# Block means of v moved by products with a shifted identity, and v's rows on other partitions

## The chip, the core and the metric

The kernel runs on one core of one Trainium2 chip. A core has five engines that run their own instruction streams: TensorE (PE, matrix products; its weight loads are listed as PEld), VectorE (DVE), ScalarE (ACT), GpSimd (POOL) and SyncE (SP), which here only issues DMA transfers. Tiles live in SBUF, which has 128 partitions; products are accumulated in PSUM banks. The metric is device time of one execution in microseconds (us), lower is better.

## The reference, cut to what matters

Three stages follow each other, for batch B = 2 and S = 768 positions.

```
attention, 8 heads of 64:
  k_sum = max of k over blocks of 32 rows      v_sum = mean of v over blocks of 32 rows   (24 blocks)
  local scores: q k^T / 8 where |i - j| < 16, else -1e9
  block scores: q k_sum^T / 8 + log 32
  a = softmax over both together;  attn = a @ [v ; v_sum]
gate:      x = attn, heads side by side (768 x 512)
           gate = sigmoid(causal depthwise convolution of x, 5 taps);  y = (gate * (x @ w_val)) @ w_out
spatial:   h = relu(y @ w_in), split into u and v;  v normalised over its 512 columns
           vs = w_spatial @ v + b;   out = (u * vs) @ w_out2
```

The change concerns `v` and `v_sum` of the attention stage: where their rows lie in SBUF, and how the means come there.

## The kernel before, in words

**Tiles.** All working tiles are "units" of 128 partitions x 1536 floats (6 KB a partition), taken from a set of 32; products use 8 PSUM banks. A pair of heads `n` (eight pairs over both batches) is worked on together, and a pair's queries in two groups of 384, so the attention has 16 steps ("ticks").

**Windows.** Queries come in 12 blocks of 64. For a block, the keys that matter are 96 rows (64 of the block and a halo of 16 at each side), followed by the 24 block means: 120 rows in all. `windows(n)` (L512) builds the k side of this by copies in SBUF, along the free dimension. `load_v(n)` (L528) builds the v side along partitions, by four DMA transfers straight from DRAM: two of 64 rows x 768 floats (192 KB each) to partitions 16 to 79, one of 16 rows x 1472 floats (92 KB) to partitions 0 to 15, and one to partitions 80 to 95. Partitions 96 to 119 take the 24 means of v, repeated for all 12 blocks.

**Means of v.** `reduce_v(m)` (L543) loads 128 blocks of 32 rows (two transfers of 512 KB, the tensor `vn`), adds them up on DVE in six halvings, lets ACT multiply by 1/32, and then moves the 128 rows of means by small DMA transfers from SBUF to SBUF (24 rows x 64 floats, fewer at a border) into a staging tile on partitions 96 to 119. It runs three times, with 18 such transfers. `put_vsum(n)` (L564) lets POOL copy a pair's means from the staging tile to its v tile, repeated for the 12 blocks (24 x 1536).

**Attention step.** `scores(t)` (L573): 24 instructions of 64x120 on PE, masking and row maximum on DVE, exponential on ACT, normalisation on POOL. `a_T(t)`: six transposes on PE, a copy on ACT. `pv(t)` (L619): 24 instructions of 120x64 on PE against the v tile; then ACT and DVE split the result into two float32r parts and run the convolution.

**The rest.** All dense products run in float32r as three products of high and low parts (`mm3`, `product`). The weights arrive as doubles in 512 KB pieces and are turned into two parts by ACT, DVE and POOL (`load64`, `split64`). `w_product` multiplies `w_out` by `w_in` ahead of use: two sets (second half of `w_in` first) of 48 products of 128x512 each ("wp"). The gate's products (`val`, 128x384) start when the first ticks of a group are done; then follow `u`, `v`, the spatial product (`s`) and the output (`r`).

**What sets the order.** The functions don't issue instructions; they record them. `ORDER` is a table of steps that sets their priority, and a planner (`plan`, L215) lays all recorded instructions out, engine by engine, by its table of costs, the sharing of units and banks, and the priority. Each engine then runs its list strictly in order, SP's DMA issues included; an instruction whose inputs are not there holds all that stand behind it on its engine. Because a helper issues every instruction, all of them carry one line number in the profile (L213); they are told apart by tile name and shape.

## Time and profile before

| | |
|---|---|
| median of 3 runs | 276.63 us (276.42 to 277.43) |
| profiled execution | 274.73 us |
| its span, from first to last instruction | 273.0 us |
| busy: PE / PEld | 250.0 us (92%) / 224.9 us (82%) |
| busy: DVE / ACT / POOL | 187.8 / 162.4 / 173.8 us |
| moved by DMA | 33.30 MB |

The profiled execution is 1.9 us under the median of the runs. In the profile, idle time of an engine counts only where the end depends on it; the chain of waits, followed back from the last instruction, says where that is. The columns of a stretch are busy time by engine, then the granted clock of TensorE as a share of its full 2.4 GHz, the mean busy share of the 16 DMA engines and the rate that they moved. A matmul's mean duration is longer than what it adds to the busy time, since matmuls overlap in the pipeline; busy time divided by the count is what one costs.

### The profile page before, as it was taken

How to read it: one execution, taken by the hardware profiler on the slowest of the kernel's cores; microseconds unless marked ns; L12 is line 12 of the kernel's file. 1: busy time of each engine (PE TensorE's matmuls, PEld its weight loads, DVE VectorE, ACT ScalarE, POOL GpSimd, SP SyncE). 2: the span in 40 equal slices, each digit the busy share in tenths (PEclk: the TensorE clock that was granted, in tenths of full speed). 3: DMA queues.
4: the chain of work that ended last, by engine and by line, in shares of the span. 5: the costliest groups of instructions: out<-in, count | busy, mean ns of one | idle time of the engine just before them, and what ended most of it. 6: DMA issues, size and time to landing. Idle time of an engine off the chain costs nothing.

```text
span 273.0 us, 5484 instructions
## 1 busy us (share of the span) xinstructions
PE 250.0 (92%) x1914; PEld 224.9 (82%) x1914; DVE 187.8 (69%) x533; ACT 162.4 (59%) x442; POOL 173.8 (64%) x202
## 2 busy tenths in 40 slices
PE   0099998797999999999999999999999999999995
PEld 0076686576999899898899999999988989999884
DVE  0797988987999987585998667564085659257200
ACT  3779979868999999977927444213062534313221
POOL 5789865795978699895554897615137595425210
PEclk9999999799999999999999999999999999999999
DMA  6999999279994000303200050000043041201112
GB/s 203 412 406 407 330 237 242 75 206 320 209 297 158 0 0 10 118 0 118 80 1 0 2 192 0 0 4 0 0 156 115 0 170 64 77 0 41 76 65 90
DMA packets 12243, 33.30 MB, mean 122 GB/s; under 512 B 2216, under 2 KB 2488, under 8 KB 12216
## 3 DMA queue, kind: packets, MB, share of 16 engines
q1 hardware_dynamic: 12184, 32.94, 37.1%
q8 instruction: 15, 0.25, 0.4%
q14 instruction: 12, 0.10, 0.1%
q0 software_dynamic: 32, 0.02, 0.1%
HBM read 29.71 MB, written 3.15 MB: 120 GB/s over the span
## 4 chain that ended last, share of the span: by engine, by line
PE 65%; DMA 19%; DVE 8%; ACT 2%; SPq 2%; issue 1%; POOL 1%; POOLq 0%
PE at_ps L213 65%; DVE at_u L213 7%; DMA at_u<-in_v_dram 6%; DMA at_u<-in_moe_w_val_dram 6%; DMA at_u<-in_vn_dram 3%; DMA at_u<-in_moe_w_in_dram 3%; ACT at_u L213 2%; SPq L213 2%; DVE sm L213 1%; POOL at_u L213 1%; DVE km L213 1%; DMA at_u<-at_u 1%; DVE nm L213 0%; ACT xl L213 0%; ACT at_ps L213 0%
## 5 line engine op out<-in xcount | busy, mean ns | idle before, releaser
L213 PE MATMUL at_ps<-at_u,at_u 128*128 128x384 f32 (+4 forms) x1818 | 241.0, 321 | 18.7 <-ACT at_u L213 14.2
L213 PEld LDWEIGHTS at_ps<-at_u,at_u 128*128 128x128 f32 (+2 forms) x1818 | 214.2, 189 | 42.3 <-ACT at_u L213 17.9
L213 POOL TENSOR_TENSOR at_u<-at_u,at_u 128x512 fp32r<-128x512 f32 (+3 forms) x84 | 111.6, 1351 | 67.4 <-ACT at_u L213 60.7
L213 ACT CAST at_u<-at_u 128x512 fp32r<-128x512 f32 (+3 forms) x84 | 51.0, 635 | 53.5 <-DVE at_u L213 48.2
L213 ACT ACTIVATE at_u<-at_u,nm 128x120 f32<-128x120 f32 x96 | 36.7, 396 | 2.0 <-DVE nm L213 2.0
L213 DVE SCALAR_TENSOR_TENSOR at_u<-at_ps,cw,at_u 128x384 f32<-128x384 f32 (+3 forms) x64 | 36.8, 602 | 0.2
L213 ACT ACTIVATE at_u<-at_ps 128x512 f32<-128x512 f32 (+1 forms) x36 | 19.0, 549 | 25.6 <-PE at_ps L213 24.2
L213 POOL TENSOR_TENSOR at_u<-at_u,sm 128x360 f32<-128x360 f32 x32 | 26.2, 842 | 10.2 <-DVE sm L213 6.4
L213 ACT COPY at_u<-at_ps 120x384 f32<-120x384 f32 (+2 forms) x45 | 20.5, 509 | 10.3 <-PE at_ps L213 10.3
L213 DVE TENSOR_TENSOR at_u<-at_u,at_u 128x384 f32<-128x384 f32 (+2 forms) x31 | 24.9, 820 | 2.4 <-DMA at_u<-in_vn_dram 1.8
L213 DVE TENSOR_TENSOR at_u<-at_ps,at_u 128x384 fp32r<-128x384 f32 (+1 forms) x26 | 14.1, 547 | 17.0 <-PE at_ps L213 15.0
L213 DVE CUSTOM_DVE_ANT_0 at_u<-at_ps,mask 128x120 f32<-128x120 f32 x96 | 20.6, 276 | 2.8 <-PE at_ps L213 2.8
L213 POOL COPY at_u<-at_u 128x320 f32<-128x320 f32 (+2 forms) x24 | 18.5, 787 | 2.1 <-DMA at_u<-at_u 1.8
L213 ACT ACTIVATE at_ps<-at_u 128x512 f32<-128x512 f32 x20 | 12.7, 639 | 11.2 <-DMA at_u<-in_moe_w_in_dram 4.4
L213 ACT ACTIVATION_READ_ACCUMULATOR at_u<-at_u,nm 128x1 f32 x96 | 19.3, 201 | 0.0
L213 DVE TENSOR_SCALAR at_u<-at_u 128x512 uint32<-128x512 uint32 (+1 forms) x21 | 13.9, 669 | 5.5 <-DMA at_u<-in_moe_w_in_dram 5.5
L213 DVE TENSOR_TENSOR at_u<-at_ps,bias 128x384 f32<-128x384 f32 x14 | 7.5, 551 | 13.2 <-PE at_ps L213 13.2
L213 DVE BATCH_NORM_STATS2 st<-at_u 128x6 f32<-128x512 f32 x12 | 8.1, 684 | 12.3 <-ACT at_u L213 12.3
L213 DVE TENSOR_TENSOR at_u<-at_u 128x256 f32<-128x256 f32 (+4 forms) x24 | 14.3, 605 | 3.2 <-DMA at_u<-in_moe_w_spatial_dram 3.0
L213 DVE SCALAR_TENSOR_TENSOR at_u<-at_ps,at_u 128x512 uint32<-128x512 uint32 x20 | 13.6, 686 | 1.3 <-ACT at_ps L213 0.3
L213 PE MATMUL at_ps<-ident,at_u 128*120 128x128 f32 x96 | 12.7, 274 | 1.1 <-POOL at_u L213 1.1
L213 PEld LDWEIGHTS at_ps<-ident,at_u 128*120 128x120 f32 x96 | 10.9, 137 | 2.4 <-POOL at_u L213 1.6
(33 smaller groups left out, 112.7 us busy)
## 6 DMA issues: line engine op xcount, KB each, us to landing
at_u<-in_moe_w_spatial_dram SPq DMA_DIRECT2D x12, 384.0 KB
at_u<-in_moe_w_in_dram SPq DMA_DIRECT2D x8, 512.0 KB
at_u<-in_moe_w_out_dram SPq DMA_DIRECT2D x8, 512.0 KB
at_u<-in_k_dram SPq DMA_DIRECT2D x8, 384.0 KB
at_u<-in_q_dram SPq DMA_DIRECT2D x8, 384.0 KB
at_u<-in_vn_dram SPq DMA_DIRECT2D x6, 512.0 KB
at_u<-in_v_dram SPq DMA_DIRECT2D x16, 192.0 KB
out_dram<-at_u SPq DMA_DIRECT2D x11, 256.0 KB
```

What stands on the lines that cost most here:

```text
L213: getattr(real, method)(*[home(x) for x in args], **{k: home(x) for k, x in kw.items()})
```

## The change

**v on other partitions.** The 64 block rows of v go to partitions 32 to 95 instead of 16 to 79. The two halos share partitions 0 to 31, alternating: the 16 rows from the block before on even partitions, the 16 from the block after on odd ones. The k windows and the masks take the same order along their columns.

**Means by products.** The small transfers go. The identity matrix `ident` (128 x 128) becomes `moves` (128 x 264), which holds it in columns 112 to 239; 120 columns of it, taken at an offset, are a shifted identity. `put_vsum` multiplies the sums of 128 blocks by such a piece, which puts the 24 rows of a head on partitions 96 to 119 of a PSUM bank (two products where a head's rows lie in two tiles, 18 in all). ACT multiplies these 24 rows by 1/32 while it copies them to SBUF, and POOL repeats them as before.

**Planner and tiles.** The recorded regions understand a step of two partitions. Three costs in the planner's table are new. There are 33 units instead of 32 (a placeholder that took one is gone). `ORDER` is new as a whole.

```diff
-NU = 32
+NU = 33
@@ ORDER (first of its lines)
-    in0 lk mask in1 lk wout in1 kw mask in0 wp wout*2 lk in1 lq score wp in1 wout wp kw wval lq kw wval in0 lk wp
+    lk wout lk kw lk kw mask wout in1*2 kw wout lk in0 wval lq in1 wout wp lq in1 mask score kw in0 wval score wp lv
...
@@ def cost
+            if rhs.dtype == F32 and outs[0].ap[0][1] > 64:
+                return 4 * cols / 2.4 + 8, None, 0, False
...
-            rate = 130 if run <= 512 else 405 if parts > 96 else 235 if parts > 64 else 215
+            rate = 130 if run <= 512 else 405 if parts > 96 else 235 if parts > 64 else 380 if parts > 16 else 210
...
-    ident = cst([P, P], F32, "ident")
+    moves = cst([P, 264], F32, "moves")
+    ident = moves[:, 112:240]
...
@@ def load_masks
-        pool.memset(ident, 0.0)
-        pool.affine_select(out=ident, in_=ident, pattern=[[-1, P]], compare_op=ALU.not_equal, fill=1.0, base=0, channel_multiplier=1)
+        pool.memset(moves, 0.0)
+        pool.affine_select(out=moves, in_=moves, pattern=[[-1, 264]], compare_op=ALU.not_equal, fill=1.0, base=112, channel_multiplier=1)
@@ def windows
-        copy("kev", kw[:, :, 16:80], kp.rearrange("p (j r) -> p j r", r=QB))
+        copy("kev", kw[:, :, 32:WK], kp.rearrange("p (j r) -> p j r", r=QB))
...
@@ def load_v
-        pool.memset(vw[0:32, :, 0, :], 0.0)
-        pool.memset(vw[64:96, :, NB - 1, :], 0.0)
+        pool.memset(vw[0:32, :, 0 :: NB - 1, :], 0.0)
         src, dst = v[b, p], vw.rearrange("p h j d -> p (h j d)")
         for h in range(2):
-            sp.dma_start(dst[16:80, h * NB * D : (h + 1) * NB * D], src[:, h * NB * D : (h + 1) * NB * D])
-        sp.dma_start(dst[0:16, D:], src[48:64, :-D])
-        sp.dma_start(dst[80:96, :-D], src[0:16, D:])
+            sp.dma_start(dst[32:WK, h * NB * D : (h + 1) * NB * D], src[:, h * NB * D : (h + 1) * NB * D])
+        sp.dma_start(dst[0:32:2, D:], src[48:64, :-D])
+        sp.dma_start(dst[1:32:2, :-D], src[0:16, D:])
@@ def reduce_v
-        mean = t[1][:, :D]
-        act.mul(mean, t[0][:, :D], 1.0 / 32)
-        r = m * P
-        while r < (m + 1) * P:
-            h, n = divmod(r, NS)
-            if h // H not in MS:
-                MS[h // H] = stage.get().rearrange("p (h d) -> p h d", d=D)
-            e = min((m + 1) * P, r - n + NS)
-            sp.dma_start(MS[h // H][WK + n : WK + n + e - r, h % H, :], mean[r - m * P : e - m * P])
-            r = e
+        MS[m] = t[0][:, :D]
@@ def put_vsum
-        need("vsum", ((2 * n + 2) * NS - 1) // P + 1)
-        need("lv", n + 1)
-        pool.tensor_copy(VW[n][WK:KW], MS[b][WK:KW, 2 * p : 2 * p + 2].unsqueeze(2).to_broadcast([NS, 2, NB, D]))
+        last = ((2 * n + 2) * NS - 1) // P
+        need("vsum", last + 1)
+        need("lv", n + 1)
+        need("mask", 2)
+        po = psum()
+        for h in range(2):
+            r = (2 * n + h) * NS
+            tiles = range(r // P, (r + NS - 1) // P + 1)
+            for m in tiles:
+                x = 16 + r - m * P
+                pe.matmul(po[:KW, h * D : (h + 1) * D], moves[:, x : x + KW], MS[m], start=m == tiles[0], stop=m == tiles[-1], skip_group_check=True)
+        st = stage.get()[WK:KW]
+        act.mul(st, po[WK:KW, : 2 * D], 1.0 / 32)
+        pool.tensor_copy(VW[n][WK:KW], st.rearrange("p (h d) -> p h d", d=D).unsqueeze(2).to_broadcast([NS, 2, NB, D]))
```

**The order on SP, at the start.** The first transfers of before (numbers in names are of units and values; `in_moe_w_in` and `in_moe_w_out` are the weights that wp multiplies):

```order
L213 DMA at_u_76_538<-in_moe_w_in_dram 128x1024
L213 DMA at_u_79_540<-in_k_dram 128x768
L213 DMA at_u_80_545<-in_moe_w_in_dram 128x1024
L213 DMA at_u_79_540<-in_k_dram 128x768
L213 DMA at_u_83_551<-in_moe_w_out_dram 128x1024
L213 DMA at_u_86_553<-in_moe_w_in_dram 128x1024
```

And now:

```order
L221 DMA at_u_73_543<-in_k_dram 128x768
L221 DMA at_u_74_545<-in_moe_w_out_dram 128x1024
L221 DMA at_u_73_543<-in_k_dram 128x768
L221 DMA at_u_79_554<-in_k_dram 128x768
L221 DMA at_u_82_559<-in_moe_w_out_dram 128x1024
L221 DMA at_u_85_564<-in_moe_w_in_dram 128x1024
```

The first product of wp needs a piece of the second half of `w_in` (the third transfer before, the sixth now) and the first of `w_out` (the fifth before, the second now).

**The order on SP, between the sums and the loads of v.** Before, the means of the first two sums (units 138 and 149) stand ahead of the fourth load of v (unit 178):

```order
L213 DMA at_u_150_759<-in_v_dram 16x1472 x2
L213 DMA at_u_164_834<-in_v_dram 64x768 x2
L213 DMA at_u_164_834<-in_v_dram 16x1472 x2
L213 DMA at_u_171_952<-in_moe_w_val_dram 128x1024
L213 DMA at_u_176_971<-in_k_dram 128x768
L213 DMA at_u_139_981<-at_u_138_733 24x64 x5
L213 DMA at_u_139_981<-at_u_138_733 8x64
L213 DMA at_u_177_1042<-in_q_dram 128x768
L213 DMA at_u_139_981<-at_u_149_814 16x64
L213 DMA at_u_139_981<-at_u_149_814 24x64 x4
L213 DMA at_u_139_981<-at_u_149_814 16x64
L213 DMA at_u_178_938<-in_v_dram 64x768 x2
```

Now nothing waits for an engine's result there; a first load of v (not shown) stands ahead of the sums' input:

```order
L221 DMA at_u_140_792<-in_vn_dram 128x1024
L221 DMA at_u_141_803<-in_vn_dram 128x1024
L221 DMA at_u_147_808<-in_vn_dram 128x1024
L221 DMA at_u_148_816<-in_vn_dram 128x1024
L221 DMA at_u_173_824<-in_v_dram 64x768 x2
L221 DMA at_u_173_824<-in_v_dram 16x1472 x2
L221 DMA at_u_182_906<-in_moe_w_val_dram 128x1024
L221 DMA at_u_184_924<-in_k_dram 128x768
L221 DMA at_u_185_939<-in_v_dram 64x768 x2
L221 DMA at_u_185_939<-in_v_dram 16x1472 x2
L221 DMA at_u_188_976<-in_v_dram 64x768 x2
L221 DMA at_u_188_976<-in_v_dram 16x1472 x2
```

**The order on PE, around the first step of `pv`** (64x64 against a v tile). Before:

```order
L213 MATMUL at_ps_207_1106<-at_u_78_584,at_u_85_614 128x512
L213 MATMUL at_ps_189_1111<-at_u_174_978,at_u_142_718 64x64 x12
L213 MATMUL at_ps_207_1106<-at_u_78_584,at_u_85_614 128x512 x3
L213 MATMUL at_ps_193_1150<-at_u_174_978,at_u_150_759 64x64 x12
L213 MATMUL at_ps_207_1106<-at_u_93_656,at_u_85_614 128x512
```

Now, with the products with `moves` that wait for the sums in units 140 and 147:

```order
L221 MATMUL at_ps_180_1054<-at_u_139_965,at_u_106_768 128x512 x3
L221 MATMUL at_ps_186_1092<-at_u_140_792,moves 120x64 x2
L221 MATMUL at_ps_191_1096<-at_u_163_995,at_u_133_586 64x64 x12
L221 MATMUL at_ps_200_1116<-at_u_97_697,at_u_76_608 128x512 x3
L221 MATMUL at_ps_186_1092<-at_u_147_808,moves 120x64
L221 MATMUL at_ps_190_1130<-at_u_147_808,moves 120x64 x2
L221 MATMUL at_ps_200_1116<-at_u_97_697,at_u_76_608 128x512
```

Nine of the 18 products with `moves` stand up to here, two more some 80 rows of the list later, and seven after the last scores.

## Rows read from the trace of the kernel before

**Rows 1.** Stretches: length, busy us (instructions) by engine, clock, DMA share, GB/s:

```profile
0.00:13.20 13.20, 0.00 (x0) 0.00 (x0) 5.68 (x9) 7.13 (x11) 8.19 (x26) 1.00 0.85 303
13.20:63.30 50.10, 44.11 (x370) 33.62 (x370) 44.60 (x159) 40.93 (x136) 39.75 (x53) 0.97 0.87 272
63.30:91.30 28.00, 27.39 (x350) 25.22 (x350) 25.78 (x90) 27.64 (x96) 21.24 (x33) 1.00 0.76 224
91.30:269.80 178.50, 178.49 (x1195) 166.02 (x1195) 111.75 (x278) 86.31 (x201) 104.62 (x93) 1.00 0.14 52
```

**Rows 2.** Chain of waits in order of time: start us, us, what:

```profile
54.13 1.68 DMA at_u<-at_u
...
58.23 4.57 DMA at_u<-in_v_dram
...
91.30 178.50 PE at_ps L213 x1191
```

**Rows 3.** PE by shape, 91.3 to 269.8: count, busy, mean ns, idle before:

```profile
L213 PE MATMUL at_ps<-at_u,at_u 128*128 128x512 f32 x276 | 66.3, 392 | 0.0
L213 PE MATMUL at_ps<-ident,at_u 128*120 128x128 f32 x48 | 6.0, 272 | 0.0
L213 PE MATMUL at_ps<-at_u,at_u 120*64 120x64 f32 x192 | 6.0, 223 | 0.0
L213 PE MATMUL at_ps<-at_u,at_u 64*64 64x120 f32 x96 | 3.5, 299 | 0.0
```

**Rows 4.** PE by shape, 13.21 to 63.33:

```profile
L213 PE MATMUL at_ps<-at_u,at_u 128*128 128x512 f32 x96 | 28.0, 438 | 14.5 <-ACT at_u L213 14.2 <-POOL at_u L213 0.2
L213 PE MATMUL at_ps<-at_u,at_u 64*64 64x120 f32 x192 | 10.0, 309 | 0.1
L213 PE MATMUL at_ps<-ident,at_u 128*120 128x128 f32 x30 | 4.2, 277 | 1.1 <-POOL at_u L213 1.1
L213 PE MATMUL at_ps<-at_u,at_u 120*64 120x64 f32 x48 | 2.6, 278 | 1.4 <-POOL at_u L213 1.4
```

**Rows 5.** SP's issues in order of time: start us, us, what, count:

```profile
44.71 5.10 SPq L213 DMA_DIRECT2D at_u<-at_u  x6
49.92 0.39 SPq L213 DMA_DIRECT2D at_u<-in_q_dram  x1
50.41 4.28 SPq L213 DMA_DIRECT2D at_u<-at_u  x6
54.79 2.28 SPq L213 DMA_DIRECT2D at_u<-in_v_dram  x4
...
64.33 10.89 SPq L213 DMA_DIRECT2D at_u<-in_v_dram  x12
```

**Rows 6.** Stretches as in rows 1, by what DMA moves in them:

```profile
8.00:24.00 16.00, 10.53 (x53) 7.73 (x54) 13.37 (x31) 13.25 (x31) 13.51 (x20) 1.00 1.02 410
...
50.40:54.80 4.40, 3.06 (x27) 2.26 (x27) 4.02 (x16) 3.84 (x18) 4.23 (x6) 0.65 0.32 96
```

**Rows 7.** Order of time on DVE, ACT, POOL and PE, from the first sum to `pv`:

```profile
35.69 2.29 DVE L213 TENSOR_TENSOR at_u<-at_u,at_u 128x1024 f32<-128x1024 f32 x1 [1.24 <-DMA at_u<-in_vn_dram]
...
41.83 0.23 DVE L213 TENSOR_TENSOR at_u<-at_u 128x64 f32<-128x64 f32 x1
42.98 0.24 ACT L213 ACTIVATE at_u<-at_u 128x64 f32<-128x64 f32 x1
50.22 2.88 POOL L213 COPY at_u<-at_u 24x1536 f32<-24x1536 f32 x2 [1.77 <-DMA at_u<-at_u]
51.74 6.19 PE L213 MATMUL at_ps<-at_u,at_u 120*64 120x64 f32 x59 [1.35 <-POOL at_u L213]
63.33 5.79 PE L213 MATMUL at_ps<-at_u,at_u 128*128 128x384 f32 x89 [2.17 <-DMA at_u<-in_v_dram]
```

**Rows 8.** Groups by shape, nearest to the new ACT instruction:

```profile
L213 ACT ACTIVATE at_u<-at_u 128x64 f32<-128x64 f32 x3 | 0.8, 259 | 0.0
L213 ACT COPY at_u<-at_ps 128x256 f32<-128x256 f32 x2 | 0.7, 373 | 1.9 <-PE at_ps L213 1.9
```

More of the change, by code (lines that the diff above doesn't have):

```diff
@@ L39 @@
 ORDER = """
-    in0 lk mask in1 lk wout in1 kw mask in0 wp wout*2 lk in1 lq score wp in1 wout wp kw wval lq kw wval in0 lk wp
-    in0 lq*2 vsum kw lv score vsum lv wp score put cw put score lv score wval at put lk lq lv wp*2 put at score pv*2
-    wval at score wp at lv pv lq at score pv wu lq kw gate lk val lv pv lv*2 kw val*2 at*2 val wu at wu score*2 lk
-    wu lk pv*2 put kw pv score*2 kw u*2 vsum gate u wv val*4 at*2 ws wv lq u at*2 wv score*4 pv wv pv u put v put v
-    at ws v at*2 u at v put pv*2 ws pv*4 gate v*2 u ws*2 u val*3 gate val*2 out2 ws val wt val*2 v out2 u*3 s*2 v s
-    v s u out2*2 s*4 u v*2 wt v r wt s*3 r s r s*3 r s u s r u*2 s*2 r s*2 r*2 s r*4
+    lk wout lk kw lk kw mask wout in1*2 kw wout lk in0 wval lq in1 wout wp lq in1 mask score kw in0 wval score wp lv
+    lq*2 in0*2 wp vsum cw put wp vsum score*2 wp*2 at score at lv put score wp wval lk lv put wu lv*2 put pv at kw
+    wp pv lv pv at score pv at gate lv at wval lq val score pv lv val*2 lq at val wv lk wv score wu pv*2 at wv kw
+    wu*2 score put lk kw lk pv gate kw wv v u val*2 u lq u score*4 lq score*2 vsum v val*2 v at u at*6 put at put*2
+    u pv*2 u v pv*5 gate pv gate ws u v*2 u ws*3 val*2 ws val ws val*2 out2 val*2 u out2 v val wt out2 s*4 u s v*3 u
+    v out2 v wt r u wt s*6 u s*2 r*2 s*2 u s r u*2 s r s*2 r*2 s*2 r s r*4
 """
@@ L83, in region @@
         size = SIZES[ap.dtype]
-        p0, f0 = divmod(ap.offset, ps)
+        row = 1
+        for n in ap.tensor.shape[1:]:
+            row *= n
+        p0, f0 = divmod(ap.offset, row)
         f1 = f0 + sum(st * (n - 1) for st, n in free) + 1
-        return ap.tensor.name, p0, p0 + pn, f0 * size, f1 * size
+        return ap.tensor.name, p0, p0 + ps // row * (pn - 1) + 1, f0 * size, f1 * size, ps // row
     def record(self, eng, real, method, args, kw):
@@ L102, in record @@
                 continue
-            name, p0, p1, f0, f1 = self.region(x)
+            name, p0, p1, f0, f1, step = self.region(x)
             touched.add(name)
@@ L106, in record @@
             for h in self.hist.get(name, []):
-                q, w, a0, a1, b0, b1 = h
+                q, w, a0, a1, b0, b1, other = h
+                if step == other == 2 and (a0 - p0) % 2:
+                    keep.append(h)
+                    continue
                 if name.startswith("ps") and q.eng != eng:
@@ L115, in record @@
                 keep.append(h)
-            keep.append((o, writes, p0, p1, f0, f1))
+            keep.append((o, writes, p0, p1, f0, f1, step))
             self.hist[name] = keep
@@ L188, in cost @@
         if method == "affine_select":
-            return 700, None, 0, True
+            return 450, None, 0, True
         two = len(big) > 1
@@ L372, in tile_kernel @@
     const = ctx.enter_context(tc.tile_pool(name="const", bufs=1))
-    units = ctx.enter_context(tc.tile_pool(name="units", bufs=1))
+    homes = ctx.enter_context(tc.tile_pool(name="homes", bufs=1))
     ps = ctx.enter_context(tc.tile_pool(name="ps", bufs=1, space=PSUM))
@@ L377, in tile_kernel @@
     uid = [0]
-    homes = ctx.enter_context(tc.tile_pool(name="homes", bufs=1))
     plan.homes["u"] = lambda i, x: homes.tile([P, 1536], x.dtype, tag=f"h{i}", name="at_" + x.name, bufs=1)
@@ L383, in unit @@
         uid[0] += 1
-        x = units.tile([P, 1536], dt, tag="u", name=f"u{uid[0]}")
+        x = homes.tile([P, 1536], dt, tag="h0", name=f"u{uid[0]}", bufs=1)
         return plan.tile(x, "u", NU)
@@ L403, in psum @@
         uid[0] += 1
-        return plan.tile(units.tile([P, 512], F32, tag="u", name=f"ps{uid[0]}"), "bank", 8)
+        return plan.tile(homes.tile([P, 512], F32, tag="h0", name=f"ps{uid[0]}", bufs=1), "bank", 8)
     plan.homes["bank"] = lambda i, x: ps.tile([P, 512], F32, tag=f"b{i}", name="at_" + x.name, bufs=1)
@@ L447, in load_masks @@
         for c in range(2):
-            x = a3[0][64 * c : 64 * c + 64, :, :WK]
-            pool.affine_select(out=x, in_=x, pattern=[[0, NI], [1, WK]], compare_op=ALU.is_gt, fill=-1e9, base=0, channel_multiplier=-1)
-            pool.affine_select(out=x, in_=x, pattern=[[0, NI], [-1, WK]], compare_op=ALU.is_gt, fill=-1e9, base=32, channel_multiplier=1)
+            x = a3[0][64 * c : 64 * c + 64]
+            for y, n, key in ((x[:, :, 32:WK], QB, 0), (x[:, :, 0:32:2], 16, -16), (x[:, :, 1:32:2], 16, QB)):
+                if key <= 0:
+                    pool.affine_select(out=y, in_=y, pattern=[[0, NI], [1, n]], compare_op=ALU.is_gt, fill=-1e9, base=16 + key, channel_multiplier=-1)
+                if key >= 0:
+                    pool.affine_select(out=y, in_=y, pattern=[[0, NI], [-1, n]], compare_op=ALU.is_gt, fill=-1e9, base=16 - key, channel_multiplier=1)
         pool.tensor_copy(added[1], added[0])
-        pool.memset(a3[0][0:64, 0, 0:16], -1e9)
-        pool.memset(a3[1][64:128, NI - 1, 80:96], -1e9)
+        pool.memset(a3[0][0:64, 0, 0:32:2], -1e9)
+        pool.memset(a3[1][64:128, NI - 1, 1:32:2], -1e9)
         yield
-        pool.memset(ident, 0.0)
-        pool.affine_select(out=ident, in_=ident, pattern=[[-1, P]], compare_op=ALU.not_equal, fill=1.0, base=0, channel_multiplier=1)
+        pool.memset(moves, 0.0)
+        pool.affine_select(out=moves, in_=moves, pattern=[[-1, 264]], compare_op=ALU.not_equal, fill=1.0, base=112, channel_multiplier=1)
         yield
```

9 lines of the change are left out of this document (4 added, 5 removed).

## The prediction

> **What bounds the kernel now.** I read the chain of waits first, from its end. Its last 178.5 us are PE without a break, from 91.3 to 269.8 [rows 2]. Then I cut the span into stretches and looked how far back PE is full [rows 1]: from 91.3 on it is busy 178.49 of 178.50 us, from 63.3 to 91.3 still 27.39 of 28.00. There DVE (25.78) and ACT (27.64) are nearly as full. So the end is set by how early PE gets full, and by how much work it then has. Only the time before 63.3 can be won by better supply.
>
> How much is lost there? The view of PE by shape gives the undisturbed price of an instruction in the full stretch [rows 3]: 66.3/276 = 0.240 us for 128x512, 6.0/48 = 0.125 for a transpose, 6.0/192 = 0.031 for 120x64, 3.5/96 = 0.036 for 64x120. The same view between 13.2 and 63.3 [rows 4] has 96, 30, 48 and 192 of them: 23.0 + 3.8 + 1.5 + 6.9 = 35 us of work in 50.1 us. Some 15 us are lost: 6.0 are shown as idle (50.10 less 44.11 [rows 1]), the rest hides in stretched instructions (0.29 us instead of 0.24 for a 128x512, by 28.0/96).
>
> Then I followed the chain there. It goes through v's loads and through the small transfers of the means [rows 2]. SP's own rows [rows 5] show how: from 44.7 to 54.7 SP spends 5.10 + 4.28 us on twelve of them and issues one other load, and the fourth load of v starts only at 54.8. In 50.4 to 54.8 the DMA engines are busy 0.32 of the time, against 1.02 from 8 to 24 [rows 6], and the granted clock is 0.65: for part of the stretch it was at 1.2 GHz, after PE had waited 1.35 us for POOL [rows 7]. That cost 4.4 x 0.35 = 1.5 us of PE's work. Finally PE waits 2.17 us for a load of v at 63.33 [rows 7].
>
> **The change part by part.**
>
> *The way of the means.* Before, the last addition of the first sum ends at 42.06, ACT scales it at 42.98, and `pv` starts at 51.74 [rows 7]: 9.7 us, most of it the queue on SP and the landing. Now the same way is two products, an ACT copy and one POOL copy. A product of 120x64 with full columns isn't in the trace. Bounds: 0.031 us (the 120x64 of `pv`) and 0.24 (a 128x512) [rows 3]; I take the transpose's 0.125, which has the nearest shape. The ACT copy lies between 0.26 and 0.37 us [rows 8]; I take 0.3. POOL's copy is 2.88/2 = 1.44 [rows 7]. With 0.25 for two products and some 0.7 for three hand-overs (my estimate; POOL to PE took 0.08 here, 51.66 to 51.74), it is 2.7 us, so 7.0 us less. Against this, one load of v now stands ahead of the input of the first sum. At the price below that is 2.1 us later. The first `pv` comes 4.9 us earlier, near 46.8.
>
> *The loads of v.* Three loads in a row (twelve transfers) take 10.89 us of issues that follow the landings, 3.63 us each [rows 5], which is 160 GB/s, while 128-partition loads move at 410 [rows 6]. Where the rows lie now isn't in the trace. Bounds: all 568 KB at 410 GB/s, 1.4 us, and 3.63 as now. I take 2.1: the 384 KB of block rows, as long as the rows of a k load, at 410 GB/s (0.96 us), and the 184 KB of halos, which stay 16 rows wide, at 160 as now (1.18). Eight loads then cost 12 us less. What PE sees of this is the 2.17 us wait.
>
> The trace shows that a load takes 3.63 us now. [...]
>
> *The start.* Before, the first product of wp waits for a piece that is fifth on SP's list, now for one that is sixth; in front of it stand 2688 KB instead of 2304. At 410 GB/s the first product comes 1.0 us later than 13.2. I price it at nothing, because the 15 us that PE loses until 63.3 hide it. If wp itself became the last to be ready, the 1.0 us would count in full.
>
> *The masks, memsets and k copies* have the same sizes in another order: nothing, POOL being idle 10 us between 13.2 and 63.3 [rows 1]. Bound: 0.5 us either way.
>
> *What gets full instead.* 4.9 us at the first `pv` and 2.17 at v's load would bring 7.1. But DVE is busy 44.60 of 50.10 us before 63.3 [rows 1] and its work stays, so PE's full stretch can't start more than 5.5 us earlier. By the new list one step of scores less stands ahead of the first gate product: its 24 x 0.036 = 0.9 us are done later, within the full stretch. Nine of the 18 products with `moves` come after that point too: 9 x 0.125 = 1.1 us. They hold PE's list until the sums are there, and behind them stand wp and `pv`. ACT gets eight copies of 0.3 and loses three of 0.26; three of the eight and one of the three fall where it is 27.64 of 28 us busy: 0.6 us.
>
> *Sum.* -5.5 + 0.9 + 1.1 + 0.6 = -2.9 us. The profiled execution took 274.73 us (273.0 of span and 1.7 around it), so it becomes 271.8. That execution lies 1.9 us under the median of the runs, 276.63; against the median, which is what will be compared, the forecast is 273.7.
>
> **The rivals.**
>
> *Nothing is won (275.3 to 278).* ACT and DVE, at 27.64 and 25.78 of 28 us, bound the ramp as a whole, and getting `pv` early only moves PE's wait behind their work; or the load of v stays at 3.63 us. For it: both engines are full from 63.3 to 91.3. Against it: before that they have 9.2 and 5.5 us free [rows 1], and the full stretch starts from what they did there. If only 2.9 us of the 5.5 arrive, 0.3 us are left and the time is 276.3.
>
> *PE is held by the sums: slower.* PE's list is in order. Before, a late sum held SP; now the product with `moves` for the second sum holds PE, and the wp products that stand behind it can't fill the gap. The price follows from DVE: in the trace the first sum's additions go from 35.69 to 42.06 with scores between them [rows 7], so a sum may take 6 us; a second one that starts after the first could hold PE 5 us. With the clock at half for a while (1.5 us, as in the dip above) that turns -2.9 into +3.6: 280.2. It decides once the hold passes some 3 us. For it: the first `pv` before needed no PE instruction in front. Against it: PE has wp products and two steps of scores ahead of that place, and the second sum's load lands only 2.6 us behind the first (1024 KB at 410 GB/s).
>
> *More is won.* The 15 us lost before 63.3 are mostly supply, and DVE's work ahead of the gate's first product is also reordered. Without DVE's cap, 7.1 us and the 1.5 us of the clock go: -8.6 + 2.6 = -6.0, or 270.6. Against it: DVE's own idle time allows it only if less of its work stands ahead.
>
> *The new order as such* could leave PE waiting after 91.3, where there is no idle time now to hide it. I see nothing in the rows for it; it is in the chance of slower.
>
> **How the numbers follow.** Differences under 0.5% (1.4 us) can't be told from no change. The forecast, 273.7, has a chance of 0.50; with a range of its own of 272.3 to 275.8 from the bounds: a load of v that stays at 3.63 us leaves 7.0 - 3.6 = 3.4 us at `pv` and keeps the wait, so -3.4 + 2.6 = -0.8; one at 1.4 changes nothing under DVE's cap; products of 0.03 or 0.24 us give -0.9 or +1.0; masks and memsets 0.5. Nothing won: 0.22. Slower: 0.18. More won: 0.10. From these: faster by over 0.5% 0.59 (the forecast but for its upper edge, and the larger gain), within 0.5% 0.23, slower 0.18. The range that should hold 8 in 10 reaches from the larger gain, 269.5, into the slower case, 279.
>
> **What would show it.** SP's list has no small transfers, and the fourth load of v is issued before 48 instead of at 54.8. Three loads of v in a row take about 6 us of issues. The first `pv` starts near 46.8, the first 128x384 near 58, with no wait for a load of v at it, and the granted clock stays at 2.4 GHz once it is there. PE's waits name DVE or ACT more often before that. From there PE is full to within 3 us of the end, some 2 us longer than before. The forecast is wrong if PE stands waiting at the products with `moves` for more than 3 us, if a load of v still takes over 3 us, or if idle time of PE shows up after 91.

## The result, and the profile after

The changed kernel takes 278.44 us (277.61 to 279.17, 9 runs), the kernel before 276.42 us (273.09 to 278.25, 9 runs beside it). The ratio is 1.0102, with a 95% interval of 1.0064 to 1.014: slower by 1.0%, where 273.7 us was forecast. The profiled execution takes 278.44 us, with a span of 276.7 us. The kernels below ran in several jobs, each beside the kernel before, whose median moved between 274.4 and 276.8 us; the ratio to it within a job (fast runs only, those at most 1.5% above the fastest of their kernel, while medians take in all) is therefore the safer number, and where the two say different things both are given.

The stretches of [rows 1] in the changed kernel, and three shorter ones (same columns):

```profile
13.20:63.30 50.10, 47.51 (x419) 37.47 (x420) 42.62 (x146) 44.48 (x140) 37.41 (x45) 1.00 0.93 321
63.30:91.30 28.00, 26.48 (x275) 22.99 (x276) 25.48 (x82) 25.55 (x83) 23.34 (x32) 1.00 0.20 68
91.30:269.80 178.50, 178.50 (x1233) 166.01 (x1232) 110.79 (x299) 87.79 (x215) 102.24 (x89) 1.00 0.17 60
...
40.00:91.30 51.30, 48.60 (x515) 41.02 (x512) 44.61 (x150) 46.07 (x151) 39.66 (x53) 1.00 0.48 156
50.00:60.00 10.00, 9.23 (x113) 7.70 (x109) 6.64 (x19) 7.93 (x21) 7.82 (x11) 1.00 0.83 278
60.00:72.00 12.00, 10.39 (x126) 8.15 (x125) 10.88 (x44) 11.91 (x44) 8.85 (x11) 1.00 0.35 103
```

PE is busy 3.4 us more than before up to 63.3, and the granted clock is 1.00 there instead of 0.97. Yet DVE is busy 2.0 us less there, and from 50 to 60 us only 6.64 of 10 us. From 60 to 72 ACT is full (11.91 of 12 us) while PE is not (10.39). After 91.3 PE is full, as before. The chain, in order of time (start, us, what):

```profile
37.28 8.42 DMA at_u<-in_k_dram
45.72 0.95 DVE km L221
...
52.12 3.53 DMA at_u<-in_k_dram
55.67 0.95 DVE km L221
...
71.86 15.16 PE at_ps L221 x173
87.05 186.32 PE at_ps L221 x1272
```

The small transfers and the wait for v have left the chain [rows 2]; two loads of k stand in it now. PE ends at 273.37 instead of 269.80, so 182.07 us of its work are left at 91.3 where 178.50 were before. SP's issues where the four loads of v stand (start us, us, what, count):

```profile
39.28 12.79 SPq L221 DMA_DIRECT2D at_u<-in_v_dram  x16
52.12 0.57 SPq L221 DMA_DIRECT2D at_u<-in_k_dram  x1
```

Four loads of v go out in one block ahead of the second load of k. PE in order of time, at its first product, the first products with `moves`, the first `pv` and the first gate product:

```profile
14.39 9.82 PE L221 MATMUL at_ps<-at_u,at_u 128*128 128x512 f32 x48 [14.39 <-ACT at_u L221]
...
44.40 1.02 PE L221 MATMUL at_ps<-at_u,moves 128*120 128x64 f32 x8
...
49.67 1.80 PE L221 MATMUL at_ps<-at_u,at_u 120*64 120x64 f32 x27
...
59.68 0.60 PE L221 MATMUL at_ps<-at_u,at_u 128*128 128x384 f32 x2
```

PE by shape over the whole run (busy us, mean ns | idle before), of the changed kernel and of the kernel before:

```profile
L221 PE MATMUL at_ps<-at_u,at_u 64*64 64x120 f32 x384 | 20.3, 308 | 0.6 <-DVE nm L221 0.3 <-DVE at_u L221 0.2
...
L221 PE MATMUL at_ps<-moves,at_u 128*120 128x128 f32 x96 | 13.3, 276 | 1.8 <-POOL at_u L221 1.0 <-DVE at_u L221 0.8
L221 PE MATMUL at_ps<-at_u,moves 128*120 128x64 f32 x36 | 4.6, 264 | 0.0
```

```profile
L213 PE MATMUL at_ps<-at_u,at_u 64*64 64x120 f32 x384 | 17.3, 305 | 0.1
```

The scores cost 3.0 us more than before, and the 18 products show as 36 instructions of 4.6/36 = 0.128 us. The group between them is the transposes; their idle time, 1.8 us here, is needed for e12.

### The profile page after: what moved, and what is told of

It reads as the page before. It is cut to its first block, busy times and chain, and to the rows that moved or that the text cites. A ratio compares the mean times of both kernels' runs of the same rounds, so it can differ in the third digit from the quotient of the medians.

```text
span 276.7 us, 5538 instructions
## 1 busy us (share of the span) xinstructions
PE 256.0 (93%) x1950; PEld 229.7 (83%) x1950; DVE 185.9 (67%) x533; ACT 165.8 (60%) x447; POOL 172.9 (62%) x198
## 4 chain that ended last, share of the span: by engine, by line
PE 78%; DMA 8%; ACT 7%; DVE 4%; SPq 1%; issue 1%; POOL 0%; ACTq 0%; DVEq 0%
PE at_ps L221 78%; ACT at_u L221 6%; DMA at_u<-in_k_dram 4%; DMA at_u<-in_moe_w_in_dram 3%; DVE at_u L221 3%; SPq L221 1%; ACT at_ps L221 1%; DVE km L221 1%; POOL at_u L221 0%; DVE sm L221 0%; DVE nm L221 0%; ACT xl L221 0%; ACTq L221 0%; DVEq L221 0%
## 5 line engine op out<-in xcount | busy, mean ns | idle before, releaser
L221 ACT ACTIVATE at_u<-at_ps 128x512 f32<-128x512 f32 (+2 forms) x44 | 21.5, 498 | 32.7 <-PE at_ps L221 31.3
L221 DVE SCALAR_TENSOR_TENSOR at_u<-at_ps,cw,at_u 128x384 f32<-128x384 f32 (+2 forms) x64 | 36.9, 610 | 0.2
L221 DVE TENSOR_TENSOR at_u<-at_u,at_u 128x384 f32<-128x384 f32 (+2 forms) x31 | 27.1, 891 | 0.4
L221 DVE CUSTOM_DVE_ANT_0 at_u<-at_ps,mask 128x120 f32<-128x120 f32 x96 | 21.9, 274 | 6.1 <-PE at_ps L221 5.3
L221 DVE TENSOR_TENSOR at_u<-at_u 128x256 f32<-128x256 f32 (+4 forms) x24 | 17.8, 745 | 0.2
L221 DVE BATCH_NORM_STATS2 st<-at_u 128x6 f32<-128x512 f32 x12 | 8.2, 687 | 11.9 <-ACT at_u L221 11.8
L221 DVE SCALAR_TENSOR_TENSOR at_u<-at_u,at_ps 128x384 f32<-128x384 f32 x16 | 8.7, 548 | 9.4 <-PE at_ps L221 8.0
L221 PE MATMUL at_ps<-moves,at_u 128*120 128x128 f32 x96 | 13.3, 276 | 1.8 <-POOL at_u L221 1.0
## 6 DMA issues: line engine op xcount, KB each, us to landing
out_dram<-at_u SPq DMA_DIRECT2D x11, 256.0 KB, 2.0
```

What stands on the lines that cost most here:

```text
L221: getattr(real, method)(*[home(x) for x in args], **{k: home(x) for k, x in kw.items()})
```

## The experiments

Two ways of changing a kernel are used. In the first the planner lays the lists out anew. In the second ("lists kept") every engine's list stays as it is, and only what an instruction does, or whether it is issued, is replaced at the end (e10, e12 to e15 and e17 then move single rows of a kept list). The second is the one that separates causes. Kernels that leave out part of the work (e1, e5, e8, e11) or move v without k and the masks (e7, e8) don't compute the reference's result; they are there for their time.

**First: is it the products, or the scores' order? (e1, e2; laid out anew)**

```diff
# e1
-        po = psum()
-                pe.matmul(po[:KW, h * D : (h + 1) * D], moves[:, x : x + KW], MS[m], ...)
-        act.mul(st, po[WK:KW, : 2 * D], 1.0 / 32)
+        for h in range(2):
+            act.mul(st[:, h * D : (h + 1) * D], MS[last][WK:KW], 1.0 / 32)
# e2, in scores
                     pe.matmul(..., qt[r, :, j], kw[r, j, :], start=True, stop=True, ...)
+                    if i or h or c:
+                        plan.ops[-1].deps.add(plan.ops[-2])
```

> The changed kernel with its table of steps, but the 18 products with the shifted identity are left out: ACT scales rows 96 to 119 of a sum straight into the staging tile, so the means are the wrong ones (two small ACT copies a pair instead of one). Theory P (the products): they run as 36 PE instructions of 0.128 us, 4.6 us of a PE that is full from 72 us on; without them the time falls by 3.5 to 4.6 us, to 273.8 to 275. Rival O (the new order of steps): the order loses the time, so it stays at 277.5 or more. Rival S (the scores, 20.3 us of PE instead of 17.3, have lost their alternation between the heads): 277.5 or more too, with 64x120 still near 20 us.

> The changed kernel, with the 12 products of a step of scores tied to each other in the order in which they are recorded, so that the two heads alternate on PE in every step. Theory P: scores are stretched because PE stands beside other work there; the time moves by less than 1 us from 278.4. Rival S (the six in a row of one head cost 3 us): 64x120 falls from 20.3 to about 17.5 us of PE and the time to 275.5 to 276.5. Rival O: no change.

Measured: e1 281.4 us (ratio 1.0189, 1.0141 to 1.0237), slower than with the products; e2 277.5 us (1.0058, 1.0029 to 1.0087), with the scores at 19.4 us. In e1 the granted clock is 0.88 from 63.3 to 91.3, where PE is idle 3.2 of the 28 us. Dropping instructions moved all lists, so e1 says nothing of the products' price. e2 lies 0.9 us under the changed kernel by medians and 1.2 by ratios, which is not clear of the two intervals, and its lists moved too: alternation may be a part, and is not the whole.

**Second: the change in the old table (e3: all of it, e4: the new places alone; laid out anew)**

```diff
-ORDER = """ lk wout lk kw ... """      # the new table
+ORDER = """ in0 lk mask in1 ... """    # the table of before
# e4 also: reduce_v and put_vsum as before, with the small transfers
```

> Layout and products of the change, but with the table of steps of the kernel before. Theory P: the products' 4.6 us remain, the better supply gives 2 to 4 us back: 276.5 to 279. Rival O (the new table of steps loses the time): 273 to 275.5, under the kernel before. Rival S: 64x120 back near 17.3 us, time 275 to 276.5.

> Only v, k and the masks in the new layout; the means go by the small transfers as before, with the table of steps of before (the planner still lays it out by its new costs, with 33 units). Theory P: the loads of v cost about 2 us instead of 3.63, the wait of 2.2 us for v goes, no products: 273 to 275.5. Rival L (the layout moves nothing that PE waits for, since SP still stands at the small transfers for 10 us): 276 to 277.

Measured: e3 280.7 us (1.0196, 1.0136 to 1.0256), e4 276.69 us (1.0006, 0.9977 to 1.0034). The old table doesn't bring the old lists back: with other durations the planner lays out others. That was the reason to keep lists.

**Third: the new lists kept, without the products (e5) and with each twice (e6)**

```diff
# e5: the product is not issued; ACT scales the sum's rows instead
+                SUB[plan.ops[-1]] = []
# e6, on the first product of a head
+                SUB[plan.ops[-1]] = [plan.ops[-1].call] * 2    # 3 for the first product of a head in two tiles
```

> The changed kernel with every engine's list as it is, but the 18 products dropped from PE's list in place (ACT scales rows 96 to 119 of a sum instead of the product, so the means are the wrong ones). In the first experiment the lists were laid out anew and the clock fell; here nothing else moves. Theory P (the products lie on a full PE): 36 x 0.128 = 4.6 us less, 273.8 to 275. Rival F (up to 91 us PE waits anyway for ACT and DVE, so only the products behind it count: 14 x 0.128 = 1.8 us): 276 to 277.2, with more idle time of PE before 91. Rival C (without them PE's load falls below what keeps the clock up): 278 or more, with a stretch at a granted clock under 1.

> The changed kernel with every list as it is, but each of the 18 products issued twice in place. Theory P: another 4.6 us, 282.5 to 283.5. Rival F: only 1.8 us from those behind 91 us, 279.8 to 281. Rival C: no gain from a steadier clock is possible, since it never falls in the changed kernel: as P or F.

Measured: e5 276.83 us (1.0063, 1.0022 to 1.0105), e6 281.83 us (1.0266, 1.0189 to 1.0344): 1.6 us less and 3.4 more than the changed kernel by medians. They are of one job and lie 5.0 us apart by medians, 5.6 by ratios, for two sets of 18 products: 2.5 to 2.8 us a set. e5 lies in the range of its rival F, e6 between theory P and rival F. PE's group in e6:

```profile
L224 PE MATMUL at_ps<-at_u,moves 128*120 128x64 f32 x72 | 8.4, 266 | 0.0
```

It grew from 4.6 to 8.4 us; most of that reached the end. Even without the products the new lists are slower than before.

**Fourth: the old lists kept, v in its new places (e7), and 16 of the 18 small transfers left out (e8: both; e11: old places)**

```diff
# e7: load_v and its memset
+            SUB[plan.ops[-1]] = [(nc.sync, "dma_start", (dst[32:WK, cs], src[:, cs]), {})]
+        SUB[plan.ops[-1]] = [(nc.sync, "dma_start", (dst[0:32:2, D:], src[48:64, :-D]), {})]
+        SUB[plan.ops[-1]] = [(nc.sync, "dma_start", (dst[1:32:2, :-D], src[0:16, D:]), {})]
# e8, e11: the transfers of means; one of each batch becomes a transfer of 24 x 512
+            SUB[plan.ops[-1]] = []
```

> The kernel before with every list as it is; only the transfers of v go to partitions 32 to 95 and, alternating, 0 to 31 (k and the masks stay, so scores and rows of v don't match). Theory of the forecast: three loads of v in a row take 6 to 7 us of issues instead of 10.89, the wait of 2.2 us for v goes, SP still stands at the small transfers: 273.5 to 275. Rival L (nothing waits for the loads as such): 275.5 to 277.

> As the one before, and of the 18 small transfers only two are left (24 x 512 from the tile of means, so the means are the wrong ones); SP's ten small issues between 44.7 and 54.7 go. No product is added. Theory of the forecast (supply is worth 5.5 us until DVE is full): 270.5 to 272.5. Rival F (ACT and DVE fill what is won): 274.5 to 276.5.

> The lists of the kernel before and v in its old places, but only two of the 18 small transfers (the means are wrong in this kernel, and only the transfers are left out). With v's new places alone the time went from 275.88 to 273.27, with both to 270.06. If the two gains add: 3.2 us, about 272.8, ratio 0.988. If v's loads at 3.63 us each are what holds SP once the transfers are gone: 1 us or less, 275 to 276. If the transfers are the whole of it: 270 to 271.

Measured: e7 273.27 us (0.9938, 0.9897 to 0.998), e8 270.06 us (0.9835, 0.9743 to 0.9927), e11 273.76 us (0.9885, 0.9825 to 0.9945). By medians the gains add: 2.6 us (e7) and 3.0 us (e11) alone, 5.8 us together (from 275.88). By ratios they are 1.7, 3.2 and 4.5 us, and the interval of e8 alone reaches from 2.0 to 7.1 us, so that they add is likely and not shown closely. In e8's profiled execution PE is full from 85.37 on, for as long and over as many products as before from 91.30 [rows 2]:

```profile
85.37 178.50 PE at_ps L216 x1191
```

What the new places do shows in the two loads of v (eight transfers) that SP issues near 32 us, in the kernel before, in e11 and in e8:

```profile
32.56 10.42 SPq L213 DMA_DIRECT2D at_u<-in_v_dram  x8
```

```profile
32.60 12.90 SPq L216 DMA_DIRECT2D at_u<-in_v_dram  x8
```

```profile
31.78 7.78 SPq L216 DMA_DIRECT2D at_u<-in_v_dram  x8
```

The three loads in a row that [rows 5] show at 64.33 are not shorter in e8 (10.81 us for 10.89; 12.65 in e7, 12.00 in e9), although the DMA engines are less busy there (0.70 from 60 to 72 us in e8, 1.00 from 66 to 75 in the kernel before); during them SP waits 4.6 us for POOL in e8 (3.1 in the kernel before):

```profile
58.63 10.81 SPq L216 DMA_DIRECT2D at_u<-in_v_dram  x12
```

**Fifth: the whole change in the old lists (e9)**

```diff
+            if (t, h) in PLACE:                      # behind a step of transposes whose sum is done
+                FIX[PLACE[t, h]] = last, plan.ops[-1], bank[:, NI * P :]
...
+            SUB[last] = [last.call] + products       # into the free columns of the transposes' bank
+            SUB[at] = [at.call, (nc.scalar, "mul", (MS[b][WK:KW, ...], po[WK:KW], 1.0 / 32), {})]
```

> The whole change (v, k windows and masks in the new places, 18 products with the shifted identity, no small transfers) in the instruction lists of the kernel before: each part is put where its old counterpart stood, and the products stand behind a step of transposes whose sum is long done. Theory L (the change of the places and the products is worth some 3 to 4 us; what loses is the new lists): 270.1 of the run with the same lists and no products, plus 1.6 to 3.4 us for products and copies as measured in the new lists, so 271.5 to 274, a ratio of 0.983 to 0.993; PE full from 85.5 to 87.5 us and the clock at 1.0. Rival S (the products and copies cost more than the supply wins, whatever the lists): 276.5 or more, a ratio above 1.0, with idle PE at the products.

Measured: 273.18 us (273.06 to 273.39), ratio 0.9886 (0.9854 to 0.9919): faster than both kernels, as theory L has it. (e9 also keeps the 32 units of before.) The stretches of e9, PE's groups, and its last piece of the chain:

```profile
40.00:91.30 51.30, 50.73 (x595) 45.60 (x594) 47.71 (x179) 49.75 (x176) 40.18 (x58) 1.00 0.60 189
...
60.00:72.00 12.00, 11.91 (x130) 11.20 (x131) 11.94 (x35) 11.46 (x35) 10.20 (x21) 1.00 0.49 160
```

```profile
L221 PE MATMUL at_ps<-at_u,at_u 64*64 64x120 f32 x384 | 18.1, 305 | 0.3 <-DVE at_u L221 0.3
...
L221 PE MATMUL at_ps<-sum,moves 128*120 128x64 f32 x36 | 4.7, 257 | 0.0
```

```profile
80.82 187.39 PE at_ps L221 x1247
```

From 40 to 91.3 DVE does 3.1 us more than in the changed kernel, ACT 3.7 and PE 2.1. e9 lies above e8, which has no products, by 3.1 us in medians and 1.4 in ratios; the two are of different jobs, and the 2.5 to 2.8 us of e5 and e6 lie between.

**Sixth: what in the new lists loses? (new lists kept but for what the diff moves)**

```diff
# e10: the second load of k of the pair goes directly behind the first
+        order.remove(b)
+        order.insert(order.index(a) + 1, b)
# e12: a step's twelve scores moved up to its first one, halves alternating;  e13: e10 and e12
# e17: e13, and both loads of k moved up until just before a load of v that stood ahead (the next pair's two as well, where they can)
```

> The changed kernel with one row of SP's list moved: the load of k that is issued at 52.12 and for which DVE waits 1.09 us stands directly behind the one issued at 37.28. Theory K (this load starves DVE between 50 and 60 us, and the scores behind it come late): that wait goes, DVE is busy over 8 of the 10 us instead of 6.64, and the time falls by 3 to 6 us, to 272.5 to 275.5. Rival (the loss of the new lists is spread over many places, and the 2.16 us that DVE waits for ACT at 53.5 stay): 0 to 1 us, 277.5 to 278.5. Rival (the load pushes the loads of v behind it by 1 us): 279 or more.

> The changed kernel, its lists kept but for PE's scores: the twelve products of each step of scores stand together and alternate between the two halves of rows, at the place of the step's first product. That leaves 22 places where scores meet other work instead of 30, and 97 changes of shape instead of 103. Theory G (PE pays for changes between the 64-row scores and the other shapes, and for scores that don't alternate): the 64x120 group falls from 20.3 us to 18 to 18.5 and the time by 2 to 3.5 us, to 275 to 276.5. Rival D (PE's busy time only hides that DVE and ACT bring its inputs late): the busy time falls, the idle time rises by as much, and the time stays within 1 us of 278.4.

> The same, and the second load of k directly behind the first as in the run before it. Theory G and the late load of k are two separate terms: they add, 273.5 to 275.5, which would be most of the way to the 273.2 of the kernel with the change in the old lists. If they are the same term seen twice: no better than the better of the two alone, 275 to 277.

> The changed kernel with grouped scores and both halves of that load of k together (276.9 us), now moved further up SP's list, ahead of the second load of v and of a piece of w_val: issued near 30 us instead of 37.45. Theory D (what the new lists lose is DVE's idle time between 40 and 91 us: 7.8 us there in the run with the load at 37.45, against 3.6 with the old lists): the wait of 1.8 us for k at 45.8 goes, DVE is busy 45 us or more of the 51.3, and the time falls by 1.5 to 3 us, to 274 to 275.4. Rival V (the load of v that is now behind it, or the buffer that k waits for, makes pv late by as much): 276.5 or more, with the wait at 53 us longer.

Measured: e10 277.27 us (1.0021, 0.9992 to 1.0049), e12 277.93 us (1.0126, 1.006 to 1.0192), e13 276.86 us (1.0101, 1.0031 to 1.0172), e17 277.25 us (1.014, 1.0079 to 1.0201). e10 gains 1.2 us by medians and 2.2 by ratios, and lies between theory K and its rival. e13 gains 1.6 us by medians and nothing by ratios, so it is not shown to be better than e10 alone. In e12 the scores fall to 17.2 us, and the idle time ahead of the transposes rises from 1.8 to 2.5 us, behind DVE:

```profile
L249 PE MATMUL at_ps<-at_u,at_u 64*64 64x120 f32 x384 | 17.2, 307 | 0.0
...
L249 PE MATMUL at_ps<-moves,at_u 128*120 128x128 f32 x96 | 13.3, 276 | 2.5 <-DVE at_u L249 1.5 <-POOL at_u L249 1.0
```

That is nearest to rival D: 3.1 us less in the scores gave 0.5 us by medians and no gain by ratios, and PE as a whole is busy only 1.5 us less (254.5 for 256.0). DVE's waits of over 1 us between 45 and 60 us, in the changed kernel, e13 and e17 (idle time and what ended it in brackets):

```profile
53.50 0.56 DVE L221 TENSOR_TENSOR at_u<-at_ps,at_u 128x384 fp32r<-128x384 f32 x1 [2.16 <-ACT at_u L221]
55.67 0.95 DVE L221 TENSOR_REDUCE km<-at_u 128x24 f32<-128x768 f32 x1 [1.09 <-DMA at_u<-in_k_dram]
```

```profile
45.75 0.95 DVE L253 TENSOR_REDUCE km<-at_u 128x24 f32<-128x768 f32 x1 [1.83 <-DMA at_u<-in_k_dram]
53.42 0.56 DVE L253 TENSOR_TENSOR at_u<-at_ps,at_u 128x384 fp32r<-128x384 f32 x1 [2.06 <-POOL at_u L253]
```

```profile
52.51 0.56 DVE L263 TENSOR_TENSOR at_u<-at_ps,at_u 128x384 fp32r<-128x384 f32 x1 [2.37 <-ACT at_u L263]
```

Moving k takes a wait for k away each time, and the wait for the first results of `pv` at 52 to 54 us stays at about 2 us. So in e17 theory D's sign came (DVE is busy 45.32 us from 40 to 91.3, after 43.49 in e13), but not its time; rival V's time did. Less idle time of DVE brought no gain by itself.

**Seventh: one thing of the new lists put into e9 (e14), and ACT relieved (e15, e16)**

```diff
# e14: e9, in each unbroken run of scores first one half of rows, then the other
+            group.sort(key=lambda o: ((o.prio - base) // 2 % 2, o.prio))
# e15 (e13) and e16 (e9): the rounding copies of wp's halves
+            if o.piece[0] in ("wv", "wu") and o.eng == "ACT":
+                o.call = (self.vector, "tensor_copy", o.call[2], {})
```

> The kernel with the whole change in the old lists (273.2 us), with one thing taken from the new ones: in each unbroken run of scores all products of one half of rows come first, then all of the other, at the same places and with the same number of changes of shape. Theory G: PE's price of a score in the full stretch goes from 0.036 to 0.040 us or more, and the time up by 1 to 2.5 us, to 274.2 to 275.7. Rival D: 273 to 273.5, since DVE and ACT, not PE, set the pace before 91 us.

> The changed kernel with grouped scores and the early load of k (276.9 us), and the eight copies of 128x512 that round the halves of wp moved from ACT (0.54 us each, four of them in a row at 68.15) to the same places of DVE's list. In all runs with the new lists PE is busy some 10.4 of the 12 us from 60 to 72 while ACT is busy 11.6 or more; with the old lists it is 11.9. Theory A (ACT, full there, hands PE its inputs late, and that is most of the 3.7 us that are left): the time falls by 1.5 to 3 us, to 274 to 275.5, and PE is busy 11 us or more there. Rival O (PE's own list stands in an order whose inputs come late whatever ACT does): within 0.7 us of 276.9, with waits for DVE or POOL in place of ACT's.

> The kernel with the whole change in the old lists (273.2 us), with the same eight copies moved from ACT to DVE. Theory A says that ACT holds nobody there, since PE is full: 272.8 to 273.5, or up to 1 us worse because DVE is at 11.94 of 12 us from 60 to 72. If ACT still sets the pace before PE is full: 271.5 to 272.5, less than the 273.2 us of the same kernel without the move.

Measured: e14 274.57 us (0.9983, 0.9943 to 1.0022), e15 283.21 us (1.0281, 1.0224 to 1.0337), e16 275.77 us (0.9993, 0.9959 to 1.0027). The scores of e14, and the copies on DVE in e15 and e16:

```profile
L243 PE MATMUL at_ps<-at_u,at_u 64*64 64x120 f32 x384 | 20.9, 305 | 0.0
```

```profile
L256 DVE CAST at_u<-at_u 128x512 fp32r<-128x512 f32 x8 | 7.0, 877 | 0.0
```

```profile
L224 DVE CAST at_u<-at_u 128x512 fp32r<-128x512 f32 x8 | 5.6, 699 | 0.0
```

Halves that don't alternate cost 2.8 us of PE, and 1.4 us of time by medians, 2.7 by ratios. Theory A falls as it was put: with less on ACT and 7.0 us more on DVE, e15 is 6.3 us slower than e13 by medians (5.0 by ratios). ACT is busy only 9.10 of the 12 us from 60 to 72 in e15, and PE 9.22, less than before the move; so a full ACT alone doesn't hold PE there. The copies on DVE are a load of their own, though, and part of the loss is the clock: from 72 to 91.3 us, where PE is idle 1.5 us, the granted clock is 0.82 (19.3 x 0.18 = 3.5 us of full clock):

```profile
72.00:91.30 19.30, 17.84 (x177) 15.51 (x175) 15.37 (x42) 12.93 (x34) 15.25 (x18) 0.82 0.24 82
```

e16 missed both of its ranges: the same move costs e9 2.6 us by medians, 3.0 by ratios, at a clock of 1.00. The two show that DVE has no room for the copies; what holds PE in the new lists they don't show.

## Why the prediction was wrong, point by point

**What failed: "the new order as such ... I see nothing in the rows for it".** The whole change takes 273.18 us in the old lists and 278.44 us in the new ones: 5.3 us by medians, 6.0 by ratios (1.0102 - 0.9886, of 276 us). It is shown by e9, and once more without products, within one job, by e5 against e8 (276.83 and 270.06; 6.3 us by ratios). What differs is the lists as the planner laid them out, its choice of units included; the two were not taken apart. The forecast took 0.9 us for one step of scores, and looked for a loss as idle time after 91.3. There is none: PE is busy 178.50 of 178.50 us. The loss is work that is not yet done at 91.3. A sign of the risk was at hand, though this is an argument and no test: the diff replaced the whole table, and with PE, DVE and ACT each near full for 50 us [rows 1] a worse fit finds no room.

**What in the lists.** Three pieces were tried. Scores that don't alternate: 1.4 us by medians in e14, only 0.5 in e12, where PE then waits for DVE and POOL. PE takes 18.1 us for the scores when the two halves of rows alternate (e9), and 20.9 when they don't (e14). The late load of k: 1.2 us by medians in e10. Both together (e13): 1.6 us. The other 3.7 us by medians, from 276.9 to 273.2, are not settled (by ratios e13 gains nothing, and all 6.0 are open).

The rows only place them. Count PE's instructions by shape and take each at its price in the full stretch ([rows 3]; 0.179 us for a 128x384 and 0.128 for a product with `moves`, from the groups in this document): this estimate gives 37.7 us of work done by 60 us in the changed kernel and in e9 alike. From 60 to 72 us it gives 7.9 us in the changed kernel, 7.8 to 8.0 in e10, e12, e13 and e17, and 11.4 to 11.8 in e8, e9, e14 and e16, which have the old lists. So of the 4.3 us of work that e9 is ahead by at 91.3, 3.9 come to show in these 12 us. The gate's products there, and ACT's exponentials of the softmax, in the changed kernel and then in e9:

```profile
L221 PE MATMUL at_ps<-at_u,at_u 128*128 128x384 f32 x25 | 5.7, 356 | 0.4 <-ACT xl L221 0.3
...
L221 ACT ACTIVATE at_u<-at_u,nm 128x120 f32<-128x120 f32 x12 | 4.8, 440 | 0.0
```

```profile
L221 PE MATMUL at_ps<-at_u,at_u 128*128 128x384 f32 x46 | 9.3, 346 | 0.1
...
L221 ACT ACTIVATE at_u<-at_u,nm 128x120 f32<-128x120 f32 x6 | 2.4, 430 | 0.0
```

The new lists put two steps of scores where the old ones put one, and half as many products of the gate. Whether what happened earlier on DVE brings this about stays open: of the 51.3 us from 40 to 91.3, DVE is idle 3.6 in e9, 6.7 in the changed kernel and 7.8 in e13, and in the three kernels with new lists shown above it waits over 2 us at the first results of `pv`. In e15 DVE has copies to do there and doesn't wait, and PE does no more from 60 to 72 (7.1 us of work); a version without that wait and without more load was not made.

**The supply was right in size.** -5.5 us, capped by DVE's idle time, was the forecast; e8 gives -5.8 by medians and -4.5 by ratios, and its full stretch starts 5.9 us earlier. The cap is borne out: up to 63.3 DVE is busy 46.84 of 50.1 us in e8, for 44.60 before [rows 1]:

```profile
13.20:63.30 50.10, 48.94 (x462) 38.60 (x463) 46.84 (x166) 46.11 (x158) 43.02 (x57) 1.00 0.94 319
```

**The loads of v.** 2.1 us a load was taken for 3.63 [rows 5]. Near 32 us, with the DMA engines full (busy share 1.03 to 1.05), a load takes 3.9 us of issues in e8 (7.78 for two) against 5.2 before and 6.5 in e11 with the old places. There the direction was right, and both sizes were too low. But the row that was priced, three loads in a row, didn't get shorter, and the four in a row of the changed kernel take 12.79 us, 3.2 each: the forecast's own sign of being wrong. The 10.89 us were not landings alone; SP waited 3.1 us of them for POOL. Nor do the new places by themselves take away the wait for v: in e7 PE still waits 2.1 us for a load; it ends before 60 us instead of at 63.33. That the total for the supply came out near is in this part luck.

**The products were mis-sized.** 1.1 us on PE (nine of 18, at 0.125) and 0.6 on ACT were taken. Each of these products shows as two instructions (36 for the 18), and those ahead of the full stretch counted as well: 36 times 0.128 is 4.6 us, of which 2.5 to 2.8 reach the end by e6 against e5 (1.4 to 3.1 by e9 against e8). That PE is held by the sums, the slower rival, didn't happen: the products start at 44.40, no sum is waited for there, and none of PE's idle time stands before them.

**The start.** 1.0 us later was forecast; 14.39 against 13.21 are 1.2 us. That it would be hidden held: by 55 us the estimate above gives 33.7 us of work in the changed kernel and in e9.

**The marks passed without the gain.** First `pv` 49.67 (forecast 46.8, before 51.74 [rows 7]), first gate product 59.68 (forecast 58), no wait for v, clock at 1.0: by these of its own signs the forecast looked fulfilled, or half so. In e9 the first `pv` is 2.2 us later than in the changed kernel, and PE ends 5.2 us sooner:

```profile
51.86 4.47 PE L221 MATMUL at_ps<-at_u,at_u 120*64 120x64 f32 x58
```

What counts is the work left behind the mark. PE by shape from 91.3 to the end, of the changed kernel and then e9:

```profile
L221 PE MATMUL at_ps<-at_u,at_u 128*128 128x384 f32 x568 | 101.8, 335 | 0.0
L221 PE MATMUL at_ps<-at_u,at_u 128*128 128x512 f32 x269 | 64.4, 392 | 0.0
...
L221 PE MATMUL at_ps<-at_u,at_u 64*64 64x120 f32 x144 | 5.8, 302 | 0.0
```

```profile
L221 PE MATMUL at_ps<-at_u,at_u 128*128 128x384 f32 x544 | 97.8, 335 | 0.0
L221 PE MATMUL at_ps<-at_u,at_u 128*128 128x512 f32 x276 | 66.4, 392 | 0.0
...
L221 PE MATMUL at_ps<-at_u,at_u 64*64 64x120 f32 x96 | 3.5, 299 | 0.0
```

4.0 - 2.0 + 2.3 = 4.3 us more are left in these three groups, of 5.2 in all (PE ends at 273.37, and in e9 at 80.82 + 187.39 = 268.21).

**The clock's dip.** 4.4 x 0.35 = 1.5 us of PE's work were read from the dip at 50.4. PE is idle 1.34 of those 4.4 us, but ahead of the dip: the granted clock is 1.00 from 50.4 to 51.6 us and 0.50 from 52.0 to 54.8, and the 3.06 us in which PE is busy, at half the clock, give the same 1.5. It stands only in the rivals, not in the sum.

**The sum again.** By medians -5.8 (supply, e8 against before) + 3.1 (products, e9 against e8) + 5.3 (lists, changed kernel against e9) = +2.6 us; by ratios -1.65% + 0.51% + 2.16% = +1.02%. Each term is the step from one run to the next, so the sum must come out: it divides the loss and tests nothing. The forecast had -5.5, 1.1 with 0.6, and 0.9 in these places.

## What to carry to other kernels

A change that comes with a new instruction order is two changes: price them apart, and test them apart by keeping one order fixed while the work in it is swapped. A milestone that comes earlier proves nothing as long as the work left behind it isn't counted, by shape and at the price of the full stretch. Where several engines are near full together, move work between them only with the other engine's measured duration at hand: relieving the one that looks full can load one that has no room (e15, e16).
